# Transposing the next chunk's normalised input with the DMA instead of TensorE, in a fused layernorm, attention and SwiGLU kernel

## The chip, the cores and the metric

The kernel runs on one core of a Trainium2 chip. The metric is the device time of one execution in microseconds (us); the profile is one further execution, recorded by the hardware profiler. Engines are named as in the profile: PE is TensorE (PEld its weight loads), DVE is VectorE, ACT is ScalarE, POOL is GpSimd, SP is SyncE. An engine's name with a q (SPq, ACTq) stands for the DMA issues of its queue.

## The reference

A parallel block over 2048 tokens of width 576: the layer norm of `x` feeds a sliding-window attention (32 heads of 18, window 256) and a gated MLP of width 4608, and both are added to `x`.

```python
x = A_x                                   # (1, 2048, 576), bfloat16
xn = _layernorm(x, axis=-1)               # no scale, no shift
# _A_ref: qkv = xn @ wqkv, 32 heads of 18; scores * 18**-0.5, 0 <= q - k < 256; softmax; @ v; @ wo
# _B_ref: (silu(xn @ w1) * (xn @ w3)) @ w2, hidden width 4608
return x + _A_ref(xn, A_wqkv, A_wo) + _B_ref(xn, B_w1, B_w3, B_w2)
```

## The kernel before

The 2048 tokens are worked through in four chunks of 512 (`NC`, `CH`), each of four tiles of 128 tokens (`TB`). A chunk has three stages.

1. **Projections** (L430): queries, keys and values from the chunk's transposed normalised input, moved into place by DMAs of the SP and ACT queues (L495). In the first chunk they belong to the prologue.
2. **Gate/up**, 36 units (`NF`). A unit is 18 matmuls (`unit_pairs`, L657): nine steps, each with one matmul on the upper and one on the lower 64 rows of the array, for 128 hidden columns of `w3` and of `w1`. Then ACT takes a tanh (L666) and DVE forms the gated product `hT` (L672, L675). Each unit has two PSUM banks out of three pairs that go round. Between the matmuls, a small planner puts the attention: score steps (L550), whose two banks `SC` ACT empties with an exp (L559), with masks by POOL (L586); and the products with the values (`pv`, L607), for two groups of heads at a time, whose results go through DVE (L616, L621, L629), POOL (L622) and DMAs (`o_pack`, L644) into `oT`.
3. **The second half**, a list of 336 items (`p2_list`): two halves of the output columns, each of 144 matmuls with `w2` per tile group (L708: nine blocks `fc` of 16), 20 matmuls with `wo` (L714), and four outputs, added to `x` by DVE (L721) and sent by SP (L723). At item 19 it takes the fourth attention product.

The weights of gate/up come in blocks of four units through three buffers (`w13`, L323), each block in six parts. SP sends a block's parts at certain matmuls of the units that follow the last use of the buffer. The weights `w2` come in blocks of 16 matmuls through four buffers (L350): SP sends the next load after the last matmul of a block.

**The transposed input.** While chunk `c` is worked on, chunk `c + 1`'s input is made ready, tile by tile: `load_x` (L299), `ln_stats` on DVE and POOL, `ln_apply` on DVE (L370: 576 columns of `xn`, and a second copy of the last 64, so that `xn` has 640 columns), and `xn_turn`. `xn_turn` is ten PE transposes of 64 x 64 blocks (L382) into the two score banks `SC` and one copy from there by DVE (L389) into `xnT[:, c % 2]`, which has five blocks of 128 rows by 512 tokens. Then `xn_swap` (L395), two DMAs of SP, writes `xnS`, the first four blocks with upper and lower 64 rows exchanged. Gate/up needs `xnT` and `xnS`, the projections need only `xnT`. For the first chunk all of that is done in the prologue, with ACT as the copier.

The table `near` gives for each tile of the next chunk the units of statistics, normalisation and turn. At a turn's unit, no score step is put just ahead of it (`if not (u in xt and n > 1)`), and the next one comes at least 5 units of the planner's clock later (8 in the first chunk), because the turn occupies the score banks. The swap is sent at item 70 of the second half.

**Order.** Every engine's instructions are one list in program order. Each operation waits, through semaphores, for the writers of what it reads and the readers of what it overwrites; SP is one such list too, so a DMA of SP that waits holds up every later DMA of SP.

Of the kernel before, what the change touches and what calls it, by code (L numbers as in the profile page):

```python
# [164 lines left out]
def bass_parallel_sum__sliding_block__glu_gated_swiglu__prompt_kernel(  # L165
# [18 lines left out]
    NC = S // CH  # L184
    TB = CH // 128
    G = H // 4
    NF = F // 128
# [8 lines left out]
    add = P.add  # L196

    with ExitStack() as es:
# [8 lines left out]
        xn = [sb(f"xn{i}", [128, 640]) for i in range(2)]  # L207
# [5 lines left out]
        xnT = sb("xnT", [128, 2, 5, CH])  # L213
# [51 lines left out]
        JOBS, SC = ((0, 1), (2, 3), (4, 5)), (6, 7)  # L265
# [17 lines left out]
        def half_bank(b):  # L283
            return PS[:, b, :].bitcast(dt.bfloat16)
# [90 lines left out]
        def xn_turn(t, banks, eng="dve"):  # L375
            i = t % 2
            c, tt = divmod(t, TB)
            for k in range(5):
                for r in range(2):
                    r0 = 64 * r  # L380
                    bv = half_bank(banks[r])[:, 64 * k:64 * k + 64]
                    add("pe", lambda e, bv=bv, r0=r0, k=k: e.transpose(  # L382
                        bv, xn[i][r0:r0 + 64, k * 128:(k + 1) * 128], ident[r0:r0 + 64, r0:r0 + 64],
                        tile_position=(r0, 0)),
                        r=[("xn", i), "ident"], **{"j" if k else "w": [("ps", banks[r])]})
            both = PS[:, banks[0]:banks[0] + 2, :].bitcast(dt.bfloat16)
            src = both[:, :, 0:320].rearrange("p r (k f) -> p k r f", f=64)
            dst = xnT[:, c % 2, :, tt * 128:(tt + 1) * 128].rearrange("p k (r f) -> p k r f", f=64)
            move = (lambda e: e.tensor_copy(dst, src)) if eng == "dve" else (lambda e: e.activation(dst, src, ACT.Copy))  # L389
            add(eng, move, r=[("ps", b) for b in banks], w=[("xnT", c % 2, tt)])  # L390

        def xn_swap(c, eng):
            for n in range(2):
# [334 lines left out]
        for t in range(TB):  # L728
# [3 lines left out]
            w=["wv"], dma="wv")  # L732
# [13 lines left out]
        for h in range(2):  # L746
            for n in range(2):
# [3 lines left out]
                    dma=f"wqk{h}", **{"j" if n else "w": [f"wqk{h}"]})  # L751
# [38 lines left out]
        for h in range(2):  # L790
# [9 lines left out]
            for n, (dst, src) in enumerate(moves):  # L800
                dealt.append(add("pool", lambda e, dst=dst, src=src: e.tensor_copy(dst, src),
                                 r=[f"wqk{h}", "wqkd"], **{"j" if n else "w": [f"wp{h}"]}))
# [21 lines left out]
                for t in (TB, TB + 1):  # L824
                    xslot[t] = load_x(t)

        PV_COST, XT_COST, PV_AFTER = 6.6, 0.8, 20

        for c in range(NC):
            NS = len(steps_of(c))  # L830
            att = [(g, s) for g in range(G) for s in range(NS)]
            near = {0: (2, 3, 5), 1: (6, 7, 9)} if c == 0 else {0: (0, 2, 4), 1: (4, 6, 8)}
            near.update({2: (15, 17, 19), 3: (23, 24, 26) if c == 0 else (24, 26, 28)})
            plan = near if c + 1 < NC else {}
            stat, apply, xt = ({v[k]: i for i, v in plan.items()} for k in range(3))
            loads = {8: (2,), 17: (3,)} if c + 1 < NC else {}
            total = 9 * NF + len(att) + 3 * PV_COST + len(xt) * XT_COST
            if c:
                total += 9 * sum(COST[kind] for kind, _ in PROJ)
            start = 20 if c == 0 else 46  # L840
# [1 line left out]
            nxt = soon = start  # L842
            clock = 0.0
# [29 lines left out]
            def spaced_step():  # L873
                nonlocal nxt, soon, clock
                score_step()
                soon = clock + 7.5
                room = last - clock - PV_COST * (3 - next_pv) - 5 * sum(v > at_u for v in xt)
                nxt = max(soon, clock + room / max(1, len(att) - done))
                clock += 1
# [19 lines left out]
            for u in range(NF):  # L899
                at_u = u  # L900
                if c == 0 and u == 0:
                    owed += 12
                if u in loads:
                    for i in loads[u]:
                        xslot[(c + 1) * TB + i] = load_x((c + 1) * TB + i)
                b0 = jobs[u] = job()
                for n in range(9):
                    if u in xt and n == 8:
                        xn_turn((c + 1) * TB + xt[u], SC)
                        clock += XT_COST  # L910
                        nxt = soon = max(nxt, clock + (8 if c == 0 else 5))
                    into = nxt - (clock + 9 - n)
                    if done < len(att) and (clock >= nxt or (n == 8 and into < 3 and clock >= soon)):
                        if not (u in xt and n > 1):
                            spaced_step()
                    op = unit_pairs(c, u, n, n + 1, b0[0])
                    clock += 1
                    if n in (3, 8):
                        owe_part(op)
                unit_tanh(u, b0[0])  # L920
                if u % 4 == 3 and u < NF - 4 and (c or u != 15):
                    owed += 6
                if next_pv in pv_ready and clock >= pv_ready[next_pv] and next_pv < 3:
                    j = next_pv
                    next_pv += 1
                    banks = job()
                    pv(c, j, banks)
                    clock += PV_COST
                    for g in (2 * j, 2 * j + 1):
                        for s in range(NS):  # L930
                            if pt_of[(c, g, s)][0] != "h":
                                free.append(pt_of[(c, g, s)])
                    later(u, lambda b=banks: (pv_out(b[0], 0), pv_out(b[1], 1), o_scale(0)))
                    later(u + 1, lambda j=j: (o_turn(2 * j, 0), o_turn(2 * j, 1), o_scale(1)))
                    later(u + 2, lambda j=j: o_turn(2 * j + 1, 0))
                    later(u + 3, lambda j=j: (o_turn(2 * j + 1, 1), o_pack(j, "sp")))
                unit_h(u, b0[0])
                for what in side.pop(u, []):
                    what()
                if u in stat:  # L940
                    t = (c + 1) * TB + stat[u]
                    for part in range(2):
                        ln_stats(t, xslot[t], part)
                if u in apply:
                    t = (c + 1) * TB + apply[u]
                    ln_apply(t, xslot[t])
                if c == 0 and u in (2, 3):
                    span_main(2, G, only=slice(0, 2) if u == 2 else slice(2, None))
                if c == 0 and u in (4, 5):
                    span_last(2, G, slice(0, 3) if u == 4 else slice(3, None))  # L950
                if c == 0 and u in (8, 9, 10, 11):
                    buf, key = ((wo, "woz"), (oT, "oTz"))[(u - 8) // 2]
                    part = buf[64:128, 4, :] if u % 2 else buf[96:128, 0:4, :]
                    add("dve", lambda e, part=part: e.memset(part.bitcast(dt.float32), 0.0), **{"j" if u % 2 else "w": [key]})
                if c == 0 and u == 13:
                    for t in range(4):
                        rows = A_wo[252 * (t // 2):252 * (t // 2) + 252, :].rearrange("(s p d) f -> p s d f", p=2, d=Dh)[t % 2, :, :, :]
                        add("sp", lambda e, t=t, rows=rows: e.dma_start(wo[0:126, t, :], rows),
                            r=["woz"], dma="wo", **{"j" if t else "w": ["wo"]})
                    add("sp", lambda e: e.dma_start(wo[0:72, 4, :], A_wo[504:576, :]), r=["woz"], j=["wo"], dma="wo")  # L960
                if c == 0 and u in (20, 22, 24, 26):
                    load_w2()
                if u == 29:
                    xs = [load_x(c * TB + tt) for tt in range(TB)]
# [9 lines left out]
            for n, item in enumerate(p2_list(c)):  # L974
                p2_item(c, item, xs)
                if n == 3:
                    for u in sorted(side):
                        for what in side.pop(u):
                            what()
                elif n == 19:  # L980
                    banks = (ring(), ring())
                    pv(c, 3, banks)
                    pv_out(banks[0], 0)
                    pv_out(banks[1], 1)
                    o_scale(0)
                    o_turn(6, 0)
                    o_turn(6, 1)
                    o_scale(1)
                    o_turn(7, 0)
                    o_turn(7, 1)  # L990
                    o_pack(3, "act")
                elif n == 70 and c + 1 < NC:
                    xn_swap(c + 1, ("sp", "sp"))
                elif n in (100, 120) and c + 2 < NC:
                    t = (c + 2) * TB + (n == 120)
                    xslot[t] = load_x(t)
# [31 lines left out]
```

## Time and profile before

| | |
|---|---|
| median of 3 runs | 571.11 us (569.49 to 572.22) |
| the profiled execution | 568.22 us, its span 566.5 us |
| granted TensorE clock | 1.000 |
| gate/up matmuls L657 | 181.6 + 151.5 us |
| second half L708, L714 | 147.6 + 24.8 us |
| PE transposes L382 | 160, in 5.0 us of PE time |
| copies L389 | 12 on DVE of 0.485 us, 4 on ACT of 0.704 us |
| DMA engines, SP and ACT queue | 59.8% of the span, 116,805 packets, 81.16 MB |

The page lists the busy time of each engine, its share of the span, and groups of instructions by line. The chain of waits follows the work that ended last back from the end: each piece is what released the one after it, so a piece of PE in it is time that PE set, and a piece of another engine or of a DMA is time in which that one set the end, whether or not PE also had something to do. The windows by stage (start of projections to start of the second half, and so on) are read off this chain: chunk 1's projections start at 147.48 us, chunk 2's at 286.33, chunk 3's at 425.85.

### The profile page before, as it was taken

The page shows a single profiled execution, that of the slowest core. Times are in us where ns is not written, and L with a number is a line of the kernel's source. Part 1 is how long each engine was busy: PE and PEld are TensorE (multiplying, and loading weights), DVE is VectorE, ACT ScalarE, POOL GpSimd, SP SyncE. Part 2 cuts the span into 40 slices and gives each one's busy share as a digit, 9 for nine tenths or more (in the row PEclk, how much of TensorE's full clock was granted, in tenths as well). Part 3 has the DMA queues.
Part 4 walks back from the last instruction along what each step waited for, and adds up shares of the span by engine and source line. Part 5 has one row for each costly group of instructions (what it writes and reads, how often), then busy time and mean ns, then how long its engine had stood idle before and what let it go on. Part 6 is the DMA issues. An engine that isn't in the chain of part 4 may idle for free.

```text
span 566.5 us, 15920 instructions
## 1 busy us (share of the span) xinstructions
PE 558.1 (99%) x6885; PEld 333.0 (59%) x6885; DVE 319.7 (56%) x598; ACT 254.1 (45%) x349; POOL 163.0 (29%) x384
## 2 busy tenths in 40 slices
PE   7999999999999999999999999999999999999998
PEld 3444455677655554567765545547776454555776
DVE  7478987610368778851047777774104567767211
ACT  4356566300176767620027676670003767666000
POOL 6323443500033444430003344443000343443000
DMA  9986969785356555468536737547653674560552
GB/s 248 201 178 154 208 156 232 159 206 156 96 137 130 132 158 151 133 158 211 150 84 140 170 86 178 138 125 192 169 153 68 137 170 111 130 163 12 137 147 64
DMA packets 118499, 83.88 MB, mean 148 GB/s; under 512 B 25909, under 2 KB 116205, under 8 KB 118429
## 3 DMA queue, kind: packets, MB, share of 16 engines
q1 hardware_dynamic: 116805, 81.16, 59.8%
q10 hardware_dynamic: 1624, 1.70, 1.2%
q8 instruction: 54, 0.88, 0.7%
q14 instruction: 16, 0.13, 0.1%
HBM read 71.29 MB, written 2.36 MB: 130 GB/s over the span
## 4 chain that ended last, share of the span: by engine, by line
PE 88%; DMA 5%; SPq 3%; DVE 2%; issue 1%; ACTq 1%; ACT 0%; POOL 0%
PE ps L657 47%; PE ps L708 21%; PE ps L430 7%; PE ps L550 6%; PE ps L714 3%; PE ps L607 3%; DMA w<-in_B_w_dram 2%; SPq L323 1%; DMA wv<-in_A_wqkv_dram 1%; DMA oT<-od 1%; DMA kv<-stage 1%; ACTq L644 1%; SPq L495 1%; DVE hT L675 0%; SPq L395 0%
## 5 line engine op out<-in xcount | busy, mean ns | idle before, releaser
L657 PE MATMUL ps<-xnT,w 64*128 64x512 bf16 x1400 | 181.6, 376 | 0.0
L657 PE MATMUL ps<-xnS,w 64*128 64x512 bf16 x1120 | 151.5, 376 | 0.0
L708 PE MATMUL ps<-w,hT 128*128 128x288 bf16 x1152 | 147.6, 287 | 0.3 <-DMA w<-in_B_w_dram 0.3
L559 ACT ACTIVATE pt<-ps 128x1024 bf16<-128x1024 f32 (+1 forms) x112 | 113.1, 1010 | 64.6 <-PE ps L550 64.3
L672 DVE SCALAR_TENSOR_TENSOR gs<-th,ps 128x512 bf16<-128x512 bf16 x144 | 98.0, 680 | 73.8 <-ACT th L666 73.0
L708 PEld LDWEIGHTS ps<-w,hT 128*128 128x128 bf16 x1152 | 111.8, 98 | 31.4 <-issue 1.7
L586 POOL TENSOR_TENSOR pt<-pt,mk 128x128 int32<-128x128 int32 (+1 forms) x199 | 80.8, 428 | 76.0 <-ACT pt L559 75.8
L675 DVE SCALAR_TENSOR_TENSOR hT<-gs,ps 128x512 bf16<-128x512 bf16 x144 | 98.9, 687 | 5.0
L657 PEld LDWEIGHTS ps<-xnT,w 64*128 64x128 bf16 x1400 | 65.3, 94 | 58.7
L666 ACT ACTIVATE th<-ps 128x512 bf16<-128x512 f32 x144 | 85.5, 594 | 27.8 <-PE ps L657 27.2
L657 PEld LDWEIGHTS ps<-xnS,w 64*128 64x128 bf16 x1120 | 54.2, 94 | 55.7
L721 DVE TENSOR_TENSOR ofin<-ps,xp 128x288 bf16<-128x288 f32 x32 | 14.6, 458 | 121.2 <-PE ps L714 121.2
L443 ACT ACTIVATE stage<-ps 128x512 bf16<-128x512 f32 x16 | 9.6, 597 | 147.0 <-PE ps L430 144.7
L586 POOL TENSOR_TENSOR hT<-hT,mk 128x128 int32<-128x128 int32 (+1 forms) x31 | 12.5, 424 | 162.5 <-ACT hT L559 162.5
L550 PE MATMUL ps<-qv,kv 64*128 64x320 bf16 (+4 forms) x528 | 51.4, 261 | 1.7 <-DVE xnT L389 0.8
L550 PEld LDWEIGHTS ps<-qv,kv 64*128 64x128 bf16 x528 | 25.5, 94 | 29.8 <-DVE xnT L389 1.5
L430 PE MATMUL ps<-xnT,wp 64*128 64x512 bf16 (+1 forms) x360 | 38.3, 355 | 0.0
L629 DVE STREAM_TRANSPOSE od<-oq 128x256 bf16<-128x256 bf16 x64 | 25.8, 427 | 6.3 <-POOL oq L622 6.3
L559 ACT ACTIVATE stage<-ps 128x1024 bf16<-128x1024 f32 x24 | 24.5, 1023 | 10.2 <-PE ps L550 10.1
L430 PEld LDWEIGHTS ps<-xnT,wp 64*128 64x128 bf16 x360 | 17.4, 94 | 15.6 <-issue 0.7
L622 POOL TENSOR_TENSOR oq<-uq,rden 128x288 bf16<-128x288 f32 x16 | 10.8, 672 | 54.4 <-DVE rden L621 54.4
L714 PE MATMUL ps<-wo,oT 128*128 128x288 bf16 x160 | 24.8, 286 | 0.4 <-DMA oT<-od 0.4
(59 smaller groups left out, 355.3 us busy)
## 6 DMA issues: line engine op xcount, KB each, us to landing
w<-in_B_w_dram SPq DMA_DIRECT2D x210, 192.0 KB, 4.0
w<-in_B_w_dram SPq DMA_DIRECT2D x72, 288.0 KB, 3.1
xp<-in_A_x_dram SPq DMA_DIRECT2D x29, 144.0 KB, 4.5
out_dram<-ofin SPq DMA_DIRECT2D x32, 72.0 KB, 1.7
xnS<-xnT SPq DMA_DIRECT2D x8, 256.0 KB, 6.0
oT<-od SPq DMA_DIRECT2D x48, 36.0 KB
pt<-in_A_wqkv_dram SPq DMA_DIRECT2D x4, 288.0 KB, 6.5
hT<-in_B_w_dram SPq DMA_DIRECT2D x6, 192.0 KB, 4.0
```

What stands on the lines that cost most here:

```text
L430: op = add("pe", lambda e, out_=out_, st=st, mv=mv, n=n, r0=r0, first=first: e.matmul(out_, st, mv, start=first, stop=(part == 1 and n == ...
L550: add("pe", lambda e, r0=r0, out_=out_, kb=kb, q0=q0, nb=nb: e.matmul(out_, kb4[r0:r0 + 64, g, kb + NV - NB, :] if kb < 0 else kv[r0:r0 + ...
L559: add("act", lambda e: e.activation(pt_slot(sl)[:, 0:w, :], PS[:, SC[0]:SC[1] + 1, 0:w].rearrange("p r q -> p q r"), ACT.Exp, scale=scale) ...
L586: add("pool", lambda e, vb=vb, mm=mm: e.tensor_tensor(vb, vb, mm, ALU.mult), r=(key if n == 0 else []) + ["mk"], **{"w" if n == 0 else "j" ...
L607: add("pe", lambda e, p=p, q=q, pr=pr, sl=sl, g=g, pos=pos, q0=q0, nb=nb, col=col, first=first, n=n: e.matmul(PS[32 * q:32 * q + VW, banks ...
L629: add("dve", lambda e: e.transpose(od[i][:, g % 2, c0:c0 + CH // 2], oq[:, c0:c0 + CH // 2]), r=["oq", "oq0"], **{"j" if half or g % 2 els ...
L657: op = add("pe", lambda e, n=n, r0=r0, r=r, k=k, src=src: e.matmul(PS[:, b0 + r, :], wt[r0:r0 + 64, k, fl * 128:(fl + 1) * 128], src, star ...
L666: add("act", lambda e: e.activation(th[i][:], PS[:, bg, :], ACT.Tanh, scale=0.5), r=[("ps", bg)], w=[("th", i)])
L672: add("dve", lambda e: e.scalar_tensor_tensor(out=gs[i][:], in0=th[i][:], scalar=1.0, in1=PS[:, bg, :], op0=ALU.add, op1=ALU.mult), r=[("t ...
L675: add("dve", lambda e: e.scalar_tensor_tensor(out=hT[:, u, :], in0=gs[i][:], scalar=0.5, in1=PS[:, bu, :], op0=ALU.mult, op1=ALU.mult), r= ...
L708: add("pe", lambda e: e.matmul(bank, hT[:, f, tt * 128:(tt + 1) * 128], w2[sl][:, k, :], start=(f == 0), stop=False), r=[("h", f), ("w2", ...
L714: add("pe", lambda e: e.matmul(bank, oT[:, k, tt * 128:(tt + 1) * 128], wo[:, k, d0:d0 + HD], start=False, stop=(k == 4)), r=[("oT", j) fo ...
```

## The change

Three edits go together. A new `xn_send` issues one DMA transpose from SP, of the whole tile `xn` (128 x 640) into the same place in `xnT`; it takes the place of `xn_turn` for all chunks but the first. The table `near` is the same for the first three chunks, and moves statistics, normalisation and send late: tile 0 to units 20, 22 and 23, tile 1 to 24, 26 and 27, tile 2 to 30, 32 and 33, tile 3 to 33, 35 and item 40 of the second half (unit 40 does not exist, so that the loop over units does not send it). The swap moves from item 70 to item 300. The planner no longer counts a cost for turns and no longer keeps score steps away from them.

```diff
+        def xn_send(t):
+            i = t % 2
+            c, tt = divmod(t, TB)
+            add("sp", lambda e: e.dma_start_transpose(
+                xnT[:, c % 2, :, tt * 128:(tt + 1) * 128], xn[i][:]),
+                r=[("xn", i)], w=[("xnT", c % 2, tt)], dma=f"xnT{tt}")
...
-        PV_COST, XT_COST, PV_AFTER = 6.6, 0.8, 20
+        PV_COST, PV_AFTER = 6.6, 20
...
-            near = {0: (2, 3, 5), 1: (6, 7, 9)} if c == 0 else {0: (0, 2, 4), 1: (4, 6, 8)}
-            near.update({2: (15, 17, 19), 3: (23, 24, 26) if c == 0 else (24, 26, 28)})
+            near = {0: (20, 22, 23), 1: (24, 26, 27), 2: (30, 32, 33), 3: (33, 35, 40)}
...
-            total = 9 * NF + len(att) + 3 * PV_COST + len(xt) * XT_COST
+            total = 9 * NF + len(att) + 3 * PV_COST
...
-                    if u in xt and n == 8:
-                        xn_turn((c + 1) * TB + xt[u], SC)
-                        clock += XT_COST
-                        nxt = soon = max(nxt, clock + (8 if c == 0 else 5))
                     into = nxt - (clock + 9 - n)
                     if done < len(att) and (clock >= nxt or (n == 8 and into < 3 and clock >= soon)):
-                        if not (u in xt and n > 1):
-                            spaced_step()
+                        spaced_step()
...
+                if u in xt:
+                    xn_send((c + 1) * TB + xt[u])
                 if u in apply:
                     t = (c + 1) * TB + apply[u]
                     ln_apply(t, xslot[t])
...
-                elif n == 70 and c + 1 < NC:
+                elif n == 40 and c + 1 < NC:
+                    xn_send((c + 1) * TB + 3)
+                elif n == 300 and c + 1 < NC:
                     xn_swap(c + 1, ("sp", "sp"))
```

## The prediction

> **What bounds the kernel now.** I read the page's busy times first, then the chain that ended last in order of time, then what the SP queue issued around the places where that chain leaves PE.
>
> ```profile
> PE 558.1 (99%) x6885; PEld 333.0 (59%) x6885; DVE 319.7 (56%) x598; ACT 254.1 (45%) x349; POOL 163.0 (29%) x384
> ...
> PE 88%; DMA 5%; SPq 3%; DVE 2%; issue 1%; ACTq 1%; ACT 0%; POOL 0%
> ```
>
> PE is the bound: 99% busy, 88% of the chain, the other engines at 56% and less. A microsecond of matmul taken away from a gap-free stretch is a microsecond gained. Next, the chain (start, length, what); L708 starts a second half, L430 starts the next chunk.
>
> ```profile
> 45.82 1.02 DVE wo L954
> 46.85 0.50 DVE xnT L389
> ...
> 47.40 0.37 PE ps L550 x4
> ...
> 105.68 2.56 PE ps L708 x20
> ...
> 116.70 6.05 DMA w<-in_B_w_dram
> ...
> 127.39 16.17 PE ps L708 x132
> 147.48 10.69 PE ps L430 x118
> ...
> 171.56 0.15 PE ps L382 x10
> ...
> 244.33 2.56 PE ps L708 x20
> ...
> 255.68 5.89 DMA w<-in_B_w_dram
> ...
> 266.24 16.17 PE ps L708 x132
> 286.33 10.69 PE ps L430 x118
> ...
> 383.43 2.56 PE ps L708 x20
> ...
> 396.46 5.08 DMA oT<-od
> ...
> 405.76 16.17 PE ps L708 x132
> 425.85 10.70 PE ps L430 x118
> ...
> 522.07 2.56 PE ps L708 x20
> ...
> 543.67 16.17 PE ps L708 x132
> ```
>
> Three things are to be seen. A turn (L382, ten small transposes) costs PE 0.15 us. One turn, in the first chunk, has a stall behind it. And in the first three chunks the chain passes from PE to a DMA in the second half, in the last chunk (no turn, no swap) it does not. The SP queue shows what lies ahead of that DMA:
>
> ```profile
> 254.13 1.33 SPq L395 DMA_DIRECT2D xnS<-xnT  x2
> 255.68 2.33 SPq L350 DMA_DIRECT2D w<-in_B_w_dram  x2
> ```
>
> The swap, placed at item 70, leaves right behind the `w2` load of item 63, and the `w2` load issued at 255.68 comes next. From the page, the usual times from issue to landing:
>
> ```profile
> w<-in_B_w_dram SPq DMA_DIRECT2D x72, 288.0 KB, 3.1
> ...
> xnS<-xnT SPq DMA_DIRECT2D x8, 256.0 KB, 6.0
> ```
>
> The load behind the swap took 5.89 us instead of 3.1 and PE waited for it.
>
> **Part 1, the turns go.** Twelve turns (four in each of three chunks) of ten transposes. In PE's timeline one starts at 171.40 and the next matmul at 171.54, so a turn is 0.145 us: 12 x 0.145 = 1.7 us, all on the path, since PE has no gap there. Cross-check: from first projection to second half, chunk 1 takes 244.33 - 147.48 = 96.85 us, chunk 2 97.10, chunk 3 without turns 96.22. The differences, 0.63 and 0.88, are 4 x 0.145 = 0.58 and a rest of 0.05 and 0.30, of which I count nothing. The twelve copies out of PSUM (L389, 0.48 us on DVE) also go. Most lie beside matmul and are worth nothing, but one does not: in chunk 0 it sits behind a 1.02 us memset on DVE (45.82), and the score step at 47.40 needs the same two banks. PE had finished its matmuls at about 46.42, so 0.98 us goes. What is late next there is nothing: the score step then needs only the exp of the step before. Part 1: 2.7 us.
>
> **Part 2, the swap moves from item 70 to item 300.** First halves of the second half, from the chain: chunk 0 takes 127.39 - 105.68 = 21.71 us, chunk 1 21.91, chunk 2 22.33, chunk 3 21.60. Chunk 0's attention products inside it are 0.32 us shorter (0.98 against 1.30), so the excess over chunk 3 is 0.43, 0.31 and 0.73: 1.47 us. Chunk 2 has the swap but no `xp` loads, so the swap, not those loads, is the cause; there it is the `oT` transfer that lands late (5.08 us). All rests of the second halves take 20.09 us, so item 300 lies where there is no such pressure: the `w2` loads issued there belong to the next chunk. The swap then leaves about 4 us before the chunk's end, and lands, by its row, 6.0 us later, some 2 us into the next chunk. The first matmul that reads `xnS` comes after the projections, some 13.5 us into the chunk (161.18 against 147.48), and the first key moves (L495) are issued about 4 us into it. Cost: nothing; were that cover gone, each us of landing beyond 17 would cost one.
>
> **Part 3, the transposes are added.** Four per chunk on SP, after units 23, 27 and 33 and at item 40. Each waits for the DVE's `xn`, written one unit earlier (item 40: some 5 us after unit 35). Behind it on SP wait weight loads. In gate/up the tightest are the parts of group 8, sent in units 24 to 26 and first read in unit 32: six units of about 2.2 us, 13 us, against a landing of 4.0. So up to 9 us of delay is hidden. Issue time: between 0.37 us (the `w2` load) and 2.29 us (the longest key move), hidden there in the same way.
>
> The second half is the tight place. The send of item 40 leaves right behind the `w2` load of item 31, exactly as the swap did behind that of item 63. A load has 5.9 us less the 0.31 that PE waited, 5.6, and lands in 3.1: it can be delayed by 2.5 to 2.6 us. The swap delayed it by 2.9. No row shows a DMA transpose. Let D be its delay of the next `w2` load. Bounds: by bytes against the swap, 160/512 x 2.9 = 0.9; by packets (640 rows of 256 B on 16 engines, at the run's mean packet time of 0.598 x 16 x 566.5 / 116,805 = 0.046 us) 1.9; by the swap's pace per piece (it has 512) 3.6; with the queue held until the transpose has landed, as long as the swap needs, 6.0. Far above, cut by element into 81,920 packets, it would be 237 us each; I price that apart. I take 1.9, because DMA time in these rows goes by packets and bytes rather than by landing. Then there is no stall, and the 1.47 us of part 2 is kept.
>
> The Trainium skill speaks against this. "VectorE: DVE Perf Modes", The three transpose paths, puts a 128 x 128 bf16 transpose at 1309 ns by DMA and 390 ns on TensorE. Five blocks would be 6.5 us by that (an estimate), and the sum would be +7.5 us instead of a gain. Its page "DMA: Bandwidth & Descriptors", Latency and other measured facts, gives 261 GB/s for a DMA transpose, which for 160 KB would be 0.6 us and leave the sum as it is. No run here shows either.
>
> **Part 4, what else moves.** Statistics and normalisation go to units 20 to 35 (1.9 us of DVE per tile: 0.45 + 0.44 + 0.21 and 0.47 + 0.34). DVE has 1.37 us of a unit's 2.2, and by the planner's arithmetic the third attention product moves from unit 28 to 25 (chunk 0: 29 to 26), so its 3.5 us of DVE work lies ahead of the last two tiles. A unit's banks are reused three units later: 0 taken, at most 0.5 us per chunk. Without turns the planner spaces score steps out slightly; nothing.
>
> **Sum.** -1.7 - 1.0 - 1.5 = -4.2 us. The profiled execution took 568.22 us, of which the span is 566.5: it becomes 564.0. That execution lies 0.5% below the median 571.11 and just under the three runs (569.49 to 572.22); I apply the difference to the median: **566.9 us**. About 0.5%, 2.9 us, is what a measurement of this kernel can tell from no change.
>
> **The rivals.** With D the general sum is -4.2 + 3 x max(0, D - 2.6). It crosses -2.9 at D = 3.0, zero at 4.0, +2.9 at 5.0.
>
> - *Slower, the queue held.* The transpose occupies the queue until it has landed, D = 6.0. Then the `w2` load of item 47 comes 3.4 us late in three chunks: 10.2 - 4.2 = +6.0, **577.1 us**. It decides from D = 4.0. For it: a transfer that must gather many rows before it can write, and no row that shows it; against it: other SBUF-to-SBUF moves do not hold weight loads that long. By the skill's 1309 ns it would be about 578.6.
> - *Even, a small stall in place of the swap's.* D = 3.6: 3 x 1.0 - 4.2, **569.9 us**. For it: a swap of 512 pieces cost 2.9.
> - *Even, half the gain.* The second half keeps its excess because `oT` now lands late beside the send, or DVE is late by 0.5 us in each chunk: 571.1 - 2.7 = **568.4 us**.
> - *The change doesn't do what it says:* the DMA is cut by element; hundreds of us. The 118,499 packets of the whole run are few beside 12 x 81,920, so it would be plain to see.
>
> **Chances.** Forecast 0.45 (all of it faster by over 0.5%), the two even cases 0.25 together, queue held 0.28, cut by element 0.02. Faster 0.45, same 0.25, slower 0.30. Range: below the forecast by the rests not counted (0.35) and the spread of runs, 565.5; above to the queue held with some more, 579. That leaves out about a tenth above and a twentieth below.
>
> **What would show it.** Right: no L382 after the first chunk's start, no PE idle near 47 us, gate/up of chunks 1 and 2 within 0.3 us of chunk 3's, first halves of the second half near 21.6 us. Wrong: PE waiting for a `w` or `oT` DMA some 6 to 12 us into a second half, a `w2` load beyond 5.7 us from issue to landing right behind a transpose, or SP held by the transposes for longer than 2.3 us each. The point that would make the forecast fail is D.

## The result, and the profile after

The change made the kernel slightly slower: 571.14 us against 569.14 us (medians of 14 runs each), a ratio of **1.0031 (1.0018 to 1.0044)**. A gain of 0.7% was forecast. The execution profiled after took 572.13 us, its span 570.4 us.

Each stage but one did what the prediction said. First the chain of waits after (start, length, what; L664 is gate/up, L715 the second half, L437 the projections):

```profile
49.02 2.21 DMA kv<-stage
51.88 3.84 PE ps L664 x18
...
112.41 2.56 PE ps L715 x20
...
133.69 16.17 PE ps L715 x132
...
153.78 10.69 PE ps L437 x118
...
250.16 2.56 PE ps L715 x20
...
271.76 16.17 PE ps L715 x132
...
291.85 10.70 PE ps L437 x118
...
388.08 2.56 PE ps L715 x20
...
409.68 16.17 PE ps L715 x132
429.77 10.69 PE ps L437 x118
...
526.00 2.56 PE ps L715 x20
...
547.61 16.17 PE ps L715 x132
```

| us | before | after |
|---|---|---|
| prologue, to the first gate/up matmul | 23.0 | 25.2 |
| gate/up of chunk 0 | 82.7 | 87.2 |
| projections and gate/up, chunks 1, 2, 3 | 96.85, 97.10, 96.22 | 96.38, 96.23, 96.23 |
| first half of the second half, chunks 0 to 3 | 21.71, 21.91, 22.33, 21.60 | 21.28, 21.60, 21.60, 21.61 |

Chunks 1 and 2 now run as chunk 3 does, in both stages, and no DMA stands in the chain of a second half any more: 2.8 us came in. Gate/up of chunk 0 lost 4.5 us, and that is the result: 1.7 us slower by these two, against 2.0 us in the medians. The prologue's 2.2 us I put down to this one execution: its code is unchanged, `wv` landed 6.39 us after its issue instead of 5.33, and the kernels below, with the same prologue, reach gate/up at 23.2 to 24.4 us.

What happened in chunk 0, first in the list of waits (us in total, times, longest), then in windows of 5 us (columns: window, length, then busy time and count of PE, PEld, DVE, ACT, POOL, then the granted TensorE clock, the DMA share and GB/s):

```profile
PE ps L557 <- DMA kv<-stage: 4.4, 1, 4.4
```

```profile
45.00:50.00 5.00, 1.87 (x18) 0.67 (x14) 4.04 (x6) 1.49 (x2) 0.46 (x1) 0.99 0.38 92
50.00:55.00 5.00, 3.73 (x20) 1.52 (x22) 0.00 (x0) 1.12 (x2) 0.73 (x2) 0.50 0.77 181
55.00:60.00 5.00, 5.00 (x108) 2.59 (x106) 3.55 (x5) 2.77 (x4) 0.87 (x2) 0.82 1.09 236
```

At 46.9 us PE reaches a score step (L557, L550 before) and waits 4.4 us for a DMA that moves keys. Behind it the granted clock is 0.50: the windows' 0.99, 0.50 and 0.82 make some 6.9 us of it, until about 56.8 us, the last 5.5 us with PE at work. The unit at 51.88 takes 3.84 us instead of 1.94; from the ninth score step to the eleventh (51.27 to 58.95 us) PE needs 7.68 us, and 4.97 us for the same work in a run without the wait (the one with keys counted per group, below), so the slow clock costs 2.7 us. Together that is 7.1 us; less the 0.6 us of turns and the 1.0 us stall that went, and less the 0.8 us that PE waited for the first step's keys before (at 28.2 us) and not in this execution, 4.7 us are left, against 4.5 found.

The transposes themselves, on SP's queue (issue time least/median/most in ns, then the DMA view's median landing in us):

```profile
L395 SPq DMA_TRANSPOSE xnT<-xn x12: 1208/1298/2239, 90.0 to 394.0; - x12
```

```profile
xnT<-xn SPq DMA_TRANSPOSE x12, 4.2
```

They take 1.3 us of SP and land in 4.2 us. The first is at 90.0 us, long after the wait, so the wait is none of their doing.

**The theory.** The score steps of chunk 0 go group by group, four to a group; groups 0 and 1 have their keys from the prologue, the keys of groups 2 to 7 are moved by SP in units 2 to 5. The ninth step is the first of group 2. Before, the turns in units 5 and 9 kept score steps away from themselves; by the planner's arithmetic the ninth step stood in unit 12, step 7. PE ran it at 51.68 us without a wait; SP issued the last four key moves from 45.47 us:

```profile
51.68 0.38 PE L550 MATMUL ps<-qv,kv 64*128 64x320 bf16 x4
```

```profile
45.47 3.36 SPq L495 DMA_DIRECT2D kv<-stage  x4
```

The last of the four starts 2.6 us after the first and, as in the chain after, lands 2.2 us after its start. By this estimate the keys were there at about 50.3 us: 1.4 us to spare, by chance. Without turns the steps follow one another unit by unit, and the ninth stands in unit 10, step 2. **The rival:** the transposes on SP, or the late normalisation on DVE, cost the time.

### The profile page after: what moved, and what is told of

Its sections match the earlier page's. It is cut to its first block, busy times and chain, and to the rows that moved or that the text cites. A ratio compares the mean times of both kernels' runs of the same rounds, so it can differ in the third digit from the quotient of the medians.

```text
span 570.4 us, 15703 instructions
## 1 busy us (share of the span) xinstructions
PE 559.3 (98%) x6765; PEld 332.0 (58%) x6765; DVE 315.2 (55%) x586; ACT 253.5 (44%) x349; POOL 163.4 (29%) x384
## 2 busy tenths in 40 slices
DMA packets 126562, 85.83 MB, mean 150 GB/s; under 512 B 33973, under 2 KB 124269, under 8 KB 126493
## 4 chain that ended last, share of the span: by engine, by line
PE 97%; DMA 2%; SPq 1%; ACT 0%; issue 0%; DVE 0%
PE ps L664 49%; PE ps L715 25%; PE ps L437 9%; PE ps L557 6%; PE ps L614 3%; PE ps L721 3%; DMA wv<-in_A_wqkv_dram 1%; SPq L502 0%; DMA kv<-stage 0%; ACT xnT L389 0%; SPq L323 0%; ACT va L486 0%; SPq L741 0%; PE ps L382 0%; DVE ofin L728 0%
## 5 line engine op out<-in xcount | busy, mean ns | idle before, releaser
L664 PE MATMUL ps<-xnT,w 64*128 64x512 bf16 x1400 | 182.3, 379 | 0.0
L664 PE MATMUL ps<-xnS,w 64*128 64x512 bf16 x1120 | 152.5, 378 | 0.0
L715 PE MATMUL ps<-w,hT 128*128 128x288 bf16 x1152 | 147.1, 286 | 0.0
L715 PEld LDWEIGHTS ps<-w,hT 128*128 128x128 bf16 x1152 | 112.1, 98 | 30.3 <-issue 1.9
L664 PEld LDWEIGHTS ps<-xnT,w 64*128 64x128 bf16 x1400 | 65.3, 95 | 61.6 <-issue 1.2
L673 ACT ACTIVATE th<-ps 128x512 bf16<-128x512 f32 x144 | 85.4, 593 | 25.4 <-PE ps L664 25.2
L664 PEld LDWEIGHTS ps<-xnS,w 64*128 64x128 bf16 x1120 | 54.0, 94 | 57.9 <-issue 1.6
L557 PE MATMUL ps<-qv,kv 64*128 64x320 bf16 (+4 forms) x528 | 51.7, 262 | 4.4 <-DMA kv<-stage 4.4
L557 PEld LDWEIGHTS ps<-qv,kv 64*128 64x128 bf16 x528 | 25.6, 95 | 32.8 <-DMA kv<-stage 4.9
L437 PE MATMUL ps<-xnT,wp 64*128 64x512 bf16 (+1 forms) x360 | 38.3, 355 | 0.0
L437 PEld LDWEIGHTS ps<-xnT,wp 64*128 64x128 bf16 x360 | 17.4, 94 | 15.6 <-issue 0.7
L437 PE MATMUL ps<-wv,xnT 64*128 64x288 bf16 x288 | 22.7, 297 | 1.7 <-DMA wv<-in_A_wqkv_dram 1.3
```

The lines of the kernel that those rows point to most:

```text
L437: op = add("pe", lambda e, out_=out_, st=st, mv=mv, n=n, r0=r0, first=first: e.matmul(out_, st, mv, start=first, stop=(part == 1 and n == ...
L557: add("pe", lambda e, r0=r0, out_=out_, kb=kb, q0=q0, nb=nb: e.matmul(out_, kb4[r0:r0 + 64, g, kb + NV - NB, :] if kb < 0 else kv[r0:r0 + ...
L664: op = add("pe", lambda e, n=n, r0=r0, r=r, k=k, src=src: e.matmul(PS[:, b0 + r, :], wt[r0:r0 + 64, k, fl * 128:(fl + 1) * 128], src, star ...
L673: add("act", lambda e: e.activation(th[i][:], PS[:, bg, :], ACT.Tanh, scale=0.5), r=[("ps", bg)], w=[("th", i)])
L715: add("pe", lambda e: e.matmul(bank, hT[:, f, tt * 128:(tt + 1) * 128], w2[sl][:, k, :], start=(f == 0), stop=False), r=[("h", f), ("w2", ...
```

## The experiments

Ratios are to the kernel before, run on the same chip, with their 95% intervals.

**The ninth step held back.** The changed kernel, one condition added:

```diff
+                    held = c == 0 and done == 2 * NS and (u, n) < (12, 7)
-                    if done < len(att) and (clock >= nxt ...
+                    if done < len(att) and not held and (clock >= nxt ...
```

> The changed kernel, with one thing undone: in the first chunk the ninth score step is held back to unit 12, step 7, where it stood before the change. My theory: that step reads key group 2 before the key moves of units 2 to 5 have landed; PE waits 4.4 us and then runs about 4 us at a granted clock of 0.50. Held back, the wait and the slow clock go, and the time is that of before less 1.6 us (turns and stall of chunk 0) less 2.8 us (gate/up of chunks 1 and 2, second halves): ratio to before 0.992 to 0.994, granted clock near 1.00 from 45 to 60 us. Rival, the late statistics and the DMA transposes themselves cost it: the ratio stays at 1.002 or above, as with the whole change.

Measured: 564.46 us, **0.9922 (0.9905 to 0.9940)**. The window where the wait was (same columns):

```profile
45.00:60.00 15.00, 14.95 (x216) 7.23 (x212) 13.86 (x26) 7.84 (x12) 4.25 (x10) 1.00 0.82 193
```

PE is busy for 14.95 of 15 us at full clock. Gate/up of chunk 0 takes 81.1 us, 1.6 less than before. One condition turns a loss of 0.3% into a gain of 0.8%, with all transposes in place: the rival falls.

**Only the turns moved, no DMA transpose.** The kernel before, with

```diff
-            near = {0: (2, 3, 5), 1: (6, 7, 9)} if c == 0 else {0: (0, 2, 4), 1: (4, 6, 8)}
-            near.update({2: (15, 17, 19), 3: (23, 24, 26) if c == 0 else (24, 26, 28)})
+            near = {0: (20, 22, 23), 1: (24, 26, 27), 2: (28, 30, 31), 3: (31, 33, 35)}
```

> The kernel before, its PE turns kept, only moved late (tile 0 to units 20, 22, 23, tile 1 to 24, 26, 27, tile 2 to 28, 30, 31, tile 3 to 31, 33, 35; the swap stays at item 70, no DMA transpose). My theory: moving the turns out of units 5 and 9 is enough to bring the ninth score step forward to unit 10, so the wait of about 4.4 us on the key moves and the slow clock behind it (about 2.2 us) are there, less the 1.0 us stall that goes: ratio 1.008 to 1.012. Rival, the transposes on the SP queue are what delays things: no such wait, ratio 0.998 to 1.000.

Measured: 589.37 us, **1.0364 (1.0339 to 1.0389)**. The waits:

```profile
PE ps L382 <- DVE xn L370: 12.6, 10, 2.2
PE ps L550 <- DMA kv<-stage: 5.4, 2, 3.5
```

The ninth step's wait is there without any DMA transpose, as the theory says: 3.5 us, and a granted clock of 0.66 in the mean of 50 to 55 us. (The other 1.9 us on keys are the first step's, for which PE waited 0.8 us in the kernel before.) The size was a miss: there is a second loss that neither theory named. PE works its list in order, and a turn placed late waits for a DVE that is behind with the normalisation: 12.6 us in ten waits, of which one of 0.8 us lies in the prologue. Behind one of them the clock fell again (PE's timeline, and a window with the columns above):

```profile
108.27 0.32 PE L382 MATMUL ps<-ident,xn 64*128 64x64 bf16 x10 [2.25 <-DVE xn L370]
```

```profile
110.00:115.00 5.00, 5.00 (x42) 2.21 (x40) 3.16 (x7) 2.55 (x4) 1.67 (x5) 0.70 0.39 100
```

The waits and the slow clock do not add up to all of the 21 us lost; the rest was not followed. With the transpose on SP the wait for DVE is SP's, and PE goes on: in the profile after, SP stood 19.3 us in all ahead of its sends, at most 4.4 us at one, and PE waited neither for them nor for the weight loads behind them. So the DMA transpose is what makes the late places affordable.

**Only the swap moved.** The kernel before, with

```diff
-                elif n == 70 and c + 1 < NC:
+                elif n == 300 and c + 1 < NC:
```

> The kernel before, with only the swap moved from item 70 to item 300. My theory: the excess of the first halves of the second half (0.43, 0.31, 0.73 us in chunks 0 to 2) is the swap's, and goes: 1.47 us, ratio 0.9974, each first half 21.6 us (chunk 0, whose attention products are shorter, 21.3). Rival, the excess comes from the x loads or the outputs: ratio 1.000.

Measured: 567.29 us, **0.9979 (0.9967 to 0.9991)**, and first halves of 21.28, 21.61, 21.60 and 21.60 us, all like the last chunk's. The excess was the swap's.

**The wait filled.** The changed kernel, with matmuls of no use just ahead of the ninth step:

```diff
+                        if c == 0 and done == 2 * NS:
+                            warm(SC[0], 20)
                         spaced_step()
```

> The changed kernel with 20 extra matmuls of 128x512 (about 4.3 us, their result is never used) put on PE just ahead of the ninth score step of chunk 0, the one that waits for the key moves. My theory: the matmuls fill the wait, so PE never idles, the granted clock stays at 1.00, and the 2.2 us of slow clock go while the 4.4 us of wait stay as filler: ratio to before 0.998 to 1.000. Rival, only the wait costs and the slow clock behind it is hidden or comes anyway: the ratio stays at 1.003. If the wait was not there in most runs, the filler adds 4.3 us: 1.010.

Measured: 568.64 us, **1.0004 (0.9992 to 1.0015)**. The same windows as above:

```profile
45.00:50.00 5.00, 5.00 (x28) 2.07 (x24) 3.04 (x5) 0.60 (x1) 0.39 (x1) 1.00 0.39 94
50.00:55.00 5.00, 5.00 (x111) 2.61 (x114) 1.93 (x3) 3.24 (x4) 1.61 (x4) 1.00 0.93 247
```

The clock stays at 1.00 where it was 0.50. The filler took 4.5 us, and the ninth step ran 26.0 us after the first gate/up matmul (26.1 with the whole change), so the wait was filled and not lengthened. The ratio is 0.0027 lower, 1.5 us where 2.2 were expected; it lies 0.0004 above the range I gave, a narrow miss. In the two profiles, gate/up of chunk 0 is 2.7 us shorter than with the whole change, as the slow clock's price above. So the wait is the larger part of the loss, the slow clock behind it the smaller.

**Keys counted per group.** Step places and order of the DMAs as changed; only what a step waits for differs. Before, each key move of groups 2 to 7 is entered as a writer of all six groups' keys, on one semaphore, so the first step of group 2 waits for the last move of all.

```diff
-                keys = [(kind, g) for g in range(a, b)]
+                keys = [(kind, g) for g in (range(a, b) if first else own[n])]
-                ... dma=f"{kind}_{a}",
+                ... dma=f"{kind}_{a}" if first else f"{kind}_{a}_{own[n][0]}",
```

(`own` lists the group of each of the last moves.)

> The changed kernel, step places and order of all DMAs as they are, but the last key moves (one per group of heads) are counted per group: a score step waits for its own group's move instead of for all of groups 2 to 7. Group 2's own move is issued about 4.5 us before the last one. If the wait of the ninth step is for moves of other groups, it goes: wait of key moves at most 0.5 us at 45 to 50 us, clock 1.00, ratio to before 0.991 to 0.994. Rival, the wait is for its own move or for the shared moves ahead of it, which land late because the queue is full: the wait stays at 2 us or more, ratio 0.998 or above.

Measured: 564.66 us, **0.9918 (0.9898 to 0.9938)**, and no wait of L558 (the same line as L557) on keys. From PE's timeline, the ninth step, and from SP's, the last key moves:

```profile
45.12 0.38 PE L558 MATMUL ps<-qv,kv 64*128 64x320 bf16 x4
```

```profile
44.82 3.36 SPq L502 DMA_DIRECT2D kv<-stage  x4
```

The step runs at 45.1 us without a gap ahead of it, when SP has just begun to issue the last key moves (until 48.2 us). So the wait was for keys that the step does not read. (Group 2's own move starts 6.5 us ahead of the last one in the profile after, 42.51 against 49.02 us, not the 4.5 that I gave.) This version is as fast as the held one, and both beat the kernel before and the changed one.

**Keys moved earlier.** The changed kernel, key moves two units earlier:

```diff
-                if c == 0 and u in (2, 3):
+                if c == 0 and u in (0, 1):
...
-                if c == 0 and u in (4, 5):
+                if c == 0 and u in (2, 3):
...
```

> The changed kernel with its early ninth score step kept, but the key moves of groups 2 to 7 issued two units earlier (units 0 to 3 instead of 2 to 5). My theory, that the step waits for these moves to land: the wait of 4.4 us shrinks to 0.5 us or less, the clock stays at 1.00, ratio to before 0.991 to 0.995. Rival, the moves are held up by the weight parts and the DMA engines, which are over 0.9 busy at 20 to 35 us, whatever their place: the wait stays above 2 us, ratio 0.999 or above.

Measured: 565.54 us, **0.9943 (0.9930 to 0.9957)**. From PE's timeline:

```profile
48.44 0.39 PE L557 MATMUL ps<-qv,kv 64*128 64x320 bf16 x4 [0.92 <-DMA kv<-stage]
```

The wait shrinks from 4.4 to 0.9 us (I had said 0.5), the clock stays at 1.00. The last moves were placed two units, 4.3 us, earlier, but SP issued them only 1.9 us earlier (19.3 us after the first gate/up matmul instead of 21.2): the weight parts are still between them. The rest is that PE came to the step 1.5 us later, after two shorter waits (0.8 us for the first step's keys, 0.4 us ahead of gate/up matmuls at 42.65 us) that the profile after does not have.

**DMA transposes at the old places.** The changed kernel with the old `near`, no send in the second half, and score steps spaced as before around the sends:

```diff
+                    if u in xt and n == 8:
+                        nxt = soon = max(nxt, clock + (8 if c == 0 else 5))
...
-                        spaced_step()
+                        if not (u in xt and n > 1):
+                            spaced_step()
...
-                elif n == 40 and c + 1 < NC:
-                    xn_send((c + 1) * TB + 3)
```

> The changed kernel, but statistics, normalisation and DMA transposes at the units at which the kernel before has them (tile 3 too, so none in the second half), and the score steps spaced around those units as before; the swap stays at item 300. My theory (only the place of the ninth score step made the change slow; the DMA transpose itself is cheap wherever it stands): no wait on key moves, ratio to before 0.991 to 0.995, as with the held step. Rival, the late places are needed because SP is crowded early in chunk 0 (key moves, weights): the key moves come later by the sends of units 5 and 9, PE waits, ratio 0.998 or above.

Measured: 565.53 us, **0.9938 (0.9925 to 0.9952)**. From the wait list, and from SP's timeline:

```profile
PE ps L557 <- DMA kv<-stage: 2.1, 1, 2.1
```

```profile
45.35 1.34 SPq L395 DMA_TRANSPOSE xnT<-xn  x1
```

The theory's range holds, but its "no wait" does not: 2.1 us remain. The last key move lands late here (its DMA is in the chain from 49.33 us, for 2.94 us), and the first send, 1.3 us, stands right ahead of the last four moves on SP, so something of the rival is true; the second send leaves only at 56.85 us, behind the step. Counted from the first gate/up matmul, the keys land 1.4 us later than before (by the estimate above), which uses up the 1.4 us that there were to spare; and PE comes to the ninth step 2.1 us earlier, because the stall, the first step's wait and two turns ahead of it are gone. The second alone would have left a wait of some 0.7 us. The clock stayed at 1.00 in spite of the wait.

**Two transposes in the second half.** The held version with tile 2's send moved there:

```diff
-            near = {0: (20, 22, 23), 1: (24, 26, 27), 2: (30, 32, 33), 3: (33, 35, 40)}
+            near = {0: (20, 22, 23), 1: (24, 26, 27), 2: (30, 32, 41), 3: (33, 35, 40)}
...
+                    xn_send((c + 1) * TB + 2)
                     xn_send((c + 1) * TB + 3)
```

> The held version with tile 2's send moved from unit 33 to item 40 of the second half, so that two DMA transposes go one behind the other there. If a transpose delays the next w2 load by about 1.5 to 2 us, as the landings of the loads behind it say, two delay it by 3 to 4, above the 2.6 us that a load can spare: 0.4 to 1.4 us in each of three chunks, ratio 0.994 to 0.997 against 0.992 with one. Rival, their cost to the queue is only SP's 1.3 us of issue: two still fit, ratio 0.992.

Measured: 565.74 us, **0.9951 (0.9934 to 0.9968)**, some 1.7 us slower than the held version, with the second half waiting for `w2`:

```profile
PEld ps L715 <- DMA w<-in_B_w_dram: 1.5, 3, 0.9
```

The first halves take 22.13, 21.60 and 21.88 us: 0.85, 0 and 0.28 more than with one, where 0.4 to 1.4 us were expected in each. The interval overlaps that of the held version, so the ratio alone decides little; the list of waits says more (0.2 us in one wait there). One transpose fits into the second half, two are at its edge.

**The swap back at item 70, behind the transpose.**

```diff
-                elif n == 300 and c + 1 < NC:
+                elif n == 70 and c + 1 < NC:
```

> The held version with the swap back at item 70, behind the transpose of item 40. It waits for that transpose to land (4.5 us from issue) and SP waits with it, so the w2 load of item 79 leaves some 4 us late and behind 512 KB: 3 to 5 us in each of three chunks, ratio 1.007 to 1.018. Rival, the swap costs what it cost before, 0.3 to 0.7 us in each: ratio 0.9948.

Measured: 567.66 us, **0.9987 (0.9969 to 1.0005)**, 3.7 us slower than the held version.

```profile
PEld ps L715 <- DMA w<-in_B_w_dram: 3.7, 6, 1.1
```

```profile
SPq L154 <- DMA xnT<-xn: 2.0, 3, 1.4
```

Both expectations missed. The first halves take 22.91, 22.15 and 22.92 us, 1.6, 0.5 and 1.3 too long: more than the swap cost without a transpose (0.4, 0.3, 0.7), far less than 3 to 5. SP stood still for the transposes for 2.0 us in all (the second list): 1.4 us in chunk 0, where the transpose landed 5.27 us after its issue began at 110.18 us, and 0.3 us in each of the other two chunks. In chunk 1 the swap left at 254.05 us, 4.2 us after the issue of the transpose began, and SP had spent most of that time on two `w2` loads that wait for PE anyway. That the rest comes from transfers one behind the other is likely, but no run shows it.

## Why the prediction was wrong, step by step

- **Part 1, the turns: right.** Gate/up of chunks 1 and 2 equals that of chunk 3 within 0.15 us (forecast: within 0.3). 0.47 and 0.87 us came in, forecast 0.58 each: in chunk 2 the rest of 0.30 that I did not count went too, in chunk 1 a little of the forecast did not come. The 0.98 us stall at 46.4 us, which I said would go with nothing late behind it, did go. For the step that had waited there, the seventh, nothing was late, as I said; two steps on, the keys were.
- **Part 2, the swap: right.** 1.47 us forecast, 0.43 + 0.31 + 0.73 found in the profile after; alone it gave a ratio of 0.9979, 1.2 us.
- **Part 3, the transposes: right in kind.** No stall follows them in the second half. I gave SP's wait for `xn` no price; it was 19.3 us in all, and PE felt none of it. In chunk 1 the `w2` load right behind the transpose landed in 4.2 us, 1.1 above the usual; the one behind tile 2's transpose and two weight parts in 5.5, 2.4 above. My D was 1.9, between the two, and below the 2.6 from which a stall begins. The 126,562 packets are 8,063 more than before, 672 for each transpose; that fits the 640 rows of 256 B that I took for D and two more packets for each of 16 engines. The Trainium skill, "VectorE: DVE Perf Modes", The three transpose paths, has 1309 ns for a 128 x 128 transpose by DMA, five times which is 6.5 us (an estimate); here a transpose of 128 x 640 took 4.2 us from issue to landing, all latency included, so the figure does not hold as a rate for this tile. The Trainium skill, "DMA: Bandwidth & Descriptors", Latency and other measured facts, has 261 GB/s, which gives 0.6 us (an estimate); the loads behind were delayed by 1.1 and 2.4 us.
- **The step that failed is in part 4:** "Without turns the planner spaces score steps out slightly; nothing." I took the mean distance of the steps. The ninth step of chunk 0 moved some two and a half units ahead, because the guard around the turns in units 5 and 9 went, and at its old place the keys had been there with only some 1.4 us to spare (an estimate). I had followed the attention products through the planner, where they moved by three units, and did not ask what the score steps need in their new places. What I put at nothing is 4.4 us of wait and 2.7 us of slow clock, against a forecast gain of 4.2.
- **The rivals:** the one that ends slower, the queue held until the transpose has landed, did not happen. None of mine named a wait for the keys. That the range held the time is luck: it reached so far up for a case that did not happen.
- **The clock.** With the wait of 4.4 us the granted clock fell to 0.50 and came back after 5.5 us of work, not the 4 that I had taken; with the one of 3.5 us it was low for some 3.4 us (0.66 in the mean of 50 to 55 us). After waits of 2.1 us (the old places), 0.9 (keys earlier) and 1.0 (before) it stayed at 1.00, but behind the wait of 2.2 us for a late turn it fell once more, for some 3.5 us (0.70 in the mean of 110 to 115 us). So these runs give no sharp limit. The Trainium skill, "TensorE: Matmul & The Clock Gate", Part 1, says that PE's clock is halved after an idle window of about 3.4 us and comes back after as long a busy one; the trace agrees in the halving after 3.5 and 4.4 us, but not after 2.2, and the clock came back after 5.5 us of work in the profile after.
- With the failed step mended, the sum comes out: 4.2 us of gain forecast, 0.9922 and 0.9918 measured, 4.4 and 4.7 us.

## What to carry to other kernels

When an operation is taken out of a hand-laid schedule, walk every later operation to its new place and ask for each when its inputs land; what looked like the cost of the removed one may have been the slack of the next. Where one wait covers several transfers, look whether the waiting work reads all of them: counting the keys per group gave the same gain as holding the step back. And work whose input may be late belongs on a queue that can wait, not on the engine that sets the time: with late PE transposes PE waited 11.8 us for DVE in gate/up, with late DMA transposes SP waited 19.3 us and PE none.

## What the runs showed of the hardware

A DMA transpose of 128 x 640 bf16 from SBUF to SBUF took 1.3 us to issue on SP, against 0.37 us for a 288 KB weight load, landed in 4.2 us, and went as 672 packets. A PE wait of 4.4 us cost 2.7 us beyond itself, because the clock stood at 0.50 for the first 5.5 us of work behind it; filled with useless matmuls, the same wait left the clock at 1.00. A wait of 2.1 us left it at 1.00 in one run, one of 2.2 us did not in another.
